# Retention and feed-forward on one core: decay tables made from the first one, and the products of rows 9 to 12 in one piece each

## Chip, cores and metric

One core of one Trainium2 chip. The metric is device time in microseconds of one execution. Engines by short names: PE (TensorE, matrix products), DVE (VectorE), ACT (ScalarE), POOL (GpSimd), SP (SyncE, which only issues transfers here).

## What is computed

The first half is a linear attention with a decaying state, the second a feed-forward layer on its result:

```python
B, H, S, D = 4, 8, 768, 64
gamma = 1.0 - 2.0 ** (-5.0 - np.arange(H))
for t in range(S):
    state = gamma * state + k[t] (outer) v[t]            # per batch and head, 64 x 64
    y[t] = (q[t] @ state) / sqrt(D)
x = y.transpose(0, 2, 1, 3).reshape(B * S, H * D)        # 3072 tokens x 512
h = x @ w_in                                             # 512 -> 2048
g = h * clip(h + 3, 0, 6) / 6
out = g @ w_out                                          # 2048 -> 512
```

The weights arrive as 64-bit floats, and the kernel makes 32-bit ones of them.

## The kernel before

**Rows.** The 3072 tokens are 24 rows of 128 tokens (6 rows per batch). The loop over time is done row by row as matrix products: scores of q and k within a row (`sc`), the product of the masked scores and v (`y`, the inner part), q times the state of the rows before (`y`, the past part), and k times v added to a running sum `uz`. The sum lies in PSUM; before it is used or goes on, ACT copies it into a tile `state` (function `keep`, L462). Decays are not applied to the state: k, v and y are multiplied by powers of gamma. Rows 0 to 7 multiply y at the end, by a table `early["dq"][:, r]` of 128 x 512 numbers (step x, L609); since y has to be multiplied by gamma to the power of the place in the batch, there are six such tables, one per row of a batch. Later rows multiply q beforehand, on POOL.

**The six tables.** The host hands in `bits`, six rows of bfloat16 parts; one PE product of 6 x 128 by 6 x 512 gives a table in PSUM (step T, L559), and ACT (tables 0, 1, 4, 5: `COPIED`) or DVE (tables 2, 3) copies it into SBUF (step C, L563 and L565). `bits` lies in the memory that the split weights of `w1` take later, so the first step that writes `w1` there (u0: ACT, L219, `w<-ww`) waits for the last product that reads `bits`.

**Rows 8 and on** are done in two halves (chunks of 64 tokens). The second half of row r-1 is added to `uz`, with the past part of that half-row's y beside it: this is step P (the first part of the products, 16 small matmuls, which the trace shows as 32). Step J is `keep(2r)`, the ACT copy of `uz`. Step Q (`chunk_rest`) is the rest: scores of row r, the inner part of row r-1, and at its end the sum of the first half of row r, which is written into `uz` again; so the end of Q can only run when J has read `uz`. Step K is `keep(2r+1)`. For rows 13 and on these run as one piece, `chunk_burst`:

```python
together(lists["add"][0], lists["past"][0])     # P
if lists["add"][0]:
    keep(2 * r)                                 # J
chunk_rest(lists)                               # Q
```

**The feed-forward layer** runs on the same PE: `h` is made of 12 matmuls of 128 x 512 per tile (step h, L505, three at a time), ACT makes relu6's first half (step r, L512), DVE the rest (step g, L516), and `g` goes to device memory (`gd`). The stores are issued from ACT's queue behind the next step r (`to_memory`, L539). There are three buffers for `g`, so a step r waits until the store of the third tile before it has landed.

**The order.** What each engine does in the first stage, about 150 us long, is written out by hand in the table `HEAD` (a letter for the step, a number for the row or tile), which `step` (L547 to L637) walks from left to right; each engine then executes its share in that order and waits on the others by semaphores. Steps a b e q f w convert a piece of the weights `w_in` (DVE, with e on ACT, L183 to L206), u and v split it into two 32-bit parts (ACT L219, DVE L222), c and d multiply v and k by decays (POOL, or four ACT activations of 128 x 64 each, L360), m masks the scores (DVE, L381), X and l split x (ACT, DVE), L and F are loads from SP's queue.

Of the kernel before, what the change touches and what calls it, by code (L numbers as in the profile page):

```python
# [20 lines left out]
P = 128  # L21
# [10 lines left out]
def retention_ffn(ctx: ExitStack, tc: tile.TileContext, qkv, w_in, w_out, dvs, dkc, dqc, dmc, tab, out, B, H, S, D):  # L32
# [22 lines left out]
    ONPOOL = (0, 1)  # L55
    COPIED = (0, 1, 4, 5)
    HEAD = """
        L0 L1 F L2 F L3 L4 O0 c0 T0 m0.0 T1 C0 T2 d0 m0.1 C1 T3 C2 N0 O1 x0 c1 U0 d1 m1.0 T4 B0 U1 a0 Y1 b0 e0 m1.1 X0
        q0 N1 f0 F L5 L6 L7 c2 O2 w0 B1 x1 d2 Y2 m2.1 u0 m2.0 U2 a1 N2 B2 l0 X1 b1 T5 C3 c3 O3 x2 d3 Y3 m3.1 m3.0 e1
        U3 l1 N3 B3 q1 C4 O4 c4 x3 f1 F Y4 d4 m4.1 m4.0 X3 U4 X2 v0 O5 B4 w1 C5 N4 l2 c5 a2 Y5 l3 d5 m5.0 x4 e2 s6  # L60
        m5.1 h0.0 c6 b2 N5 f2 d6 q2 F h0.0 u1 m6 p6 x5 h0.0 A6 X4 v1 S7 c7 w2 h0.0 a3 X5 m7 h0.1 u2 b3 l5 y6 h0.1 v2
        B6 e3 q3 p7 h0.1 l4 A7 d7 h0.1 f3 F h0.2 x6 r0.0 w3 i7 X6 u3 y7 h0.2 x7 h0.2 g0.0 X7 v3 h0.2 r0.1 l6 B7 h0.3
        l7 L8 h0.3 a4 h1.0 b4 e4 g0.1 h1.0 r0.2 q4 h1.0 f4 F h1.0 w4 h1.1 g0.2 u4 h0.3 a5 r1.0 v4 h1.1 g1.0 h0.3 b5
        h0.4 r0.3 q5 h0.4 e5 h0.4 f5 F h0.4 g0.3 Q8 L9 w5 a6 h1.1 K8 b6 r0.4 q6 h1.1 u5 P9 e6 h1.2 r1.1 h1.2 J9 g1.1
        h1.2 m8 h1.2 f6 F h1.3 v5 h1.3 w6 h1.3 g0.4 u6 h1.3 r1.2 v6 h1.4 r1.3 a7 h1.4 b7 e7 Q9 g1.2 q7 g1.3 h1.4 f7 F
        h1.4 w7 h1.5 a8 u7 b8 h1.5 e8 q8 h1.5 K9 f8 F L10 r1.4 h0.5 g1.4 h1.5 v7 h1.6 w8 h0.5 a9 u8 h0.5 b9 r1.5 q9
        h0.5 v8 h1.6 g1.5 h1.6 h1.6 P10 r1.6 h1.7 e9 h0.6 J10 f9 F r0.5 h0.6 m9 h1.7 g0.5 h0.6 g1.6 h1.7 w9 h1.7 a10
        b10 h0.6 r1.7 q10 h0.7 u9 e10 Q10 v9 r0.6 f10 F w10 h1.8 a11 u10 h0.7 b11 X8 q11 h0.7 e11 g1.7 h0.7 K10 g0.6
        X9 h1.8 v10 r0.7 h1.8 f11 F L11 h0.8 w11 h0.8 g0.7 h1.8 a12 l8 h0.8 r1.8 h0.8 g1.8 h1.9 r0.8 h1.9 u11 g0.8 e12
        h1.9 v11 h1.9 f12 P11 m10 h1.10 b12 h1.10 q12 F h1.10 l9 h1.10 w12 h1.11 a13 u12 b13 h1.11 J11 v12 r1.9 h1.11  # L70
        e13 g1.9 h1.11 r1.10 q13 Q11 f13 F L12 g1.10 w13 h1.12 X10 m11 h0.9 K11 u13 l10 h1.12 a14 h0.9 b14 e14 q14
        h0.9 r1.11 f14 h1.12 g1.11 P12 v13 h1.12 J12 w14 h0.9 a15 h0.10 u14 b15 r1.12 h0.10 e15 v14 h0.10 r0.9 h0.10
        g1.12 h0.11 r0.10 q15 h0.11 f15 h0.11 g0.9 h0.11 w15 h0.12 g0.10 u15 h0.12 r0.11 v15 h0.12 g0.11 h0.12 Q12
        r0.12 g0.12 h0.13 K12 m12 X11 h0.13 l11 h0.13 h0.13 h0.14 r0.13 h0.14 g0.13 h0.14 h0.14 h0.15 r0.14 h0.15
        g0.14 h0.15 h0.15 h1.13 r0.15 h1.13 g0.15 h1.13 h1.13 h1.14 r1.13 h1.14 g1.13 h1.14 h1.14 h1.15 r1.14 h1.15
        g1.14 h1.15 h1.15 r1.15 g1.15
    """
    BUFS = {"lkt": 1, "lqt": 2, "lvn": 2, "lkn": 1}
    SPARE = ("lkn", "lkt", "lqt", "lqt")
# [462 lines left out]
    def head():  # L542
# [4 lines left out]
        def step(kind, *a):  # L547
            r = a[0] if a else 0
            if kind == "L":
                load(r)  # L550
                if r == AHEAD:
                    nc.sync.dma_start(out=cmask, in_=dmc)
                if r < AHEAD:
                    rows[r]["dq"] = early["dq"][:, r % ROWS_B]
            elif kind == "F":
                fetched.append(fetch(w_in[len(fetched)], 2))
            elif kind == "T":
                tables[r] = ps_h.tile([P, UT], F32, tag="h", name=nm("t"))
                nc.tensor.matmul(tables[r], bits[:, 0:P], bits[:, P + r * UT : P + (r + 1) * UT], start=True, stop=True)  # L559
            elif kind == "C":  # L560
                to, src = early["dq"][:, r].rearrange("p a n -> p (a n)"), tables.pop(r)
                if r in COPIED:
                    nc.scalar.activation(out=to, in_=src, func=AF.Copy)  # L563
                else:
                    nc.vector.tensor_copy(out=to, in_=src)  # L565
            elif kind == "z":
                if "spare" not in both:
                    both["spare"] = h_bank()
                for _ in range(r):
                    nc.tensor.matmul(both["spare"][:, 0:BLK], mask[:, 0], mask, start=True, stop=True)  # L570
            elif kind == "O":
                whole_scores(r)
            elif kind == "N":
                whole_inner(r)
            elif kind == "Y":
                whole_past(r)
            elif kind == "U":
                whole_sums(r)
            elif kind == "s":
                together(*scores(r))  # L580
            elif kind == "S":
                for pair in zip(scores(r), inners(r - 1)):
                    together(*pair)
            elif kind == "i":
                for todo in inners(r):
                    together(todo)
            elif kind in "py":
                sums(r, "py".index(kind), "qt")
            elif kind in "AB":
                keep(2 * r + 1 + "AB".index(kind))  # L590
            elif kind == "P":
                lists = later(r)
                together(lists["add"][0], lists["past"][0])
            elif kind == "Q":
                chunk_rest(later(r))
            elif kind in "JK":
                keep(2 * r + "JK".index(kind))
            elif kind in "cd":
                decay(r, "cd".index(kind))
            elif kind == "m":  # L600
                if r < WHOLE:
                    whole_weigh(*a)
                elif r < AHEAD:
                    weigh(r, r % 2, tri)
                else:
                    weigh(r, 0, cmask)
            elif kind == "x":
                t = rows[r]["x"] = apool.tile([P, NPAIR, P], F32, tag="xr", name=nm("xr"))
                nc.vector.tensor_tensor(out=t, in0=both["y"][:, r % 2], in1=rows[r]["dq"], op=ALU.mult)  # L609
            elif kind == "X":  # L610
                high(x_place(r)[0], rows[r]["x"] if r < AHEAD else both["y"][:, r % 2])
            elif kind == "l":
                low(x_place(r)[1], x_place(r)[0], rows[r]["x"] if r < AHEAD else both["y"][:, r % 2])
                del rows[r]
            elif kind in "abeqf":
                if r not in conv:
                    conv[r] = conversion(fetched[r])
                conv[r][kind]()
# [203 lines left out]
def constants(H, S, D):  # L822
# [89 lines left out]
```

## Time and profile before

| | |
|---|---|
| device time, three runs | 571.28, 571.71, 572.10 us (median 571.71) |
| the profiled execution | 572.05 us, of it 570.3 us span |
| PE busy | 563.5 us, 99% of the span |
| DVE / ACT / POOL busy | 429.6 / 249.2 / 44.2 us |
| chain that ended last, by engine | PE 94%, DVE 3%, DMA 1% |

The chain that ended last is the list of pieces of work, followed back from the last instruction, each of which released the next; a microsecond can be won where it is in this chain. The first 52 us are the only stretch where engines other than PE are in it for long.

### The profile page before, as it was taken

The page shows a single profiled execution, that of the slowest core. Times are in us where ns is not written, and L with a number is a line of the kernel's source. Part 1 is how long each engine was busy: PE and PEld are TensorE (multiplying, and loading weights), DVE is VectorE, ACT ScalarE, POOL GpSimd, SP SyncE. Part 2 cuts the span into 40 slices and gives each one's busy share as a digit, 9 for nine tenths or more (in the row PEclk, how much of TensorE's full clock was granted, in tenths as well). Part 3 has the DMA queues.
Part 4 walks back from the last instruction along what each step waited for, and adds up shares of the span by engine and source line. Part 5 has one row for each costly group of instructions (what it writes and reads, how often), then busy time and mean ns, then how long its engine had stood idle before and what let it go on. Part 6 is the DMA issues. An engine that isn't in the chain of part 4 may idle for free.

```text
span 570.3 us, 11862 instructions
## 1 busy us (share of the span) xinstructions
PE 563.5 (99%) x4832; PEld 462.6 (81%) x4832; DVE 429.6 (75%) x594; ACT 249.2 (44%) x388; POOL 44.2 (8%) x50
## 2 busy tenths in 40 slices
PE   8999999999999999999999999999999999999997
PEld 6777888888888888888888888888888888888885
DVE  5879879942777678887737989679776698676881
ACT  4863434532444443444434654444335443344430
POOL 3001110220111111122000000000000000000000
PEclk9999999999999999999999999999999999999999
DMA  8946787762656666667543485565744747636611
GB/s 314 369 140 220 232 278 228 259 227 92 220 206 223 216 223 215 231 231 260 165 161 115 150 292 189 175 226 167 263 165 132 240 162 258 206 115 189 213 75 74
DMA packets 60626, 115.68 MB, mean 203 GB/s; under 512 B 6166, under 2 KB 6934, under 8 KB 60572
## 3 DMA queue, kind: packets, MB, share of 16 engines
q1 hardware_dynamic: 46304, 89.54, 47.8%
q10 hardware_dynamic: 14268, 25.39, 11.7%
q8 instruction: 38, 0.62, 0.5%
q14 instruction: 16, 0.13, 0.1%
HBM read 83.45 MB, written 31.46 MB: 201 GB/s over the span
## 4 chain that ended last, share of the span: by engine, by line
PE 94%; DVE 3%; DMA 1%; ACT 0%; issue 0%; SPq 0%; DVEq 0%
PE h L505 45%; PE o L782 40%; PE uz L458 3%; PE y L458 3%; PE sc L458 2%; DMA early<-in_qkv 1%; DMA st<-in_w_in 1%; DVE we L200 1%; DVE x L222 0%; DVE am L381 0%; DVE w L222 0%; DVE g L516 0%; DVE wb L187 0%; DVE xr L609 0%; DVE wb L195 0%
## 5 line engine op out<-in xcount | busy, mean ns | idle before, releaser
L505 PE MATMUL h<-x,w 128*128 128x512 f32 x1152 | 270.1, 393 | 0.2
L505 PEld LDWEIGHTS h<-x,w 128*128 128x128 f32 x1152 | 213.9, 188 | 46.4 <-DVE w L222 0.6
L782 PE MATMUL o<-gc,w 128*128 128x512 f32 x1008 | 228.6, 389 | 0.0
L782 PEld LDWEIGHTS o<-gc,w 128*128 128x128 f32 x1008 | 189.2, 188 | 39.3
L512 ACT ACTIVATE g<-h,three 128x512 f32<-128x512 f32 x96 | 65.8, 687 | 109.7 <-PE h L505 81.1
L516 DVE SCALAR_TENSOR_TENSOR g<-g,h 128x512 f32<-128x512 f32 x96 | 65.5, 684 | 56.2 <-ACT g L512 56.0
L219 ACT ACTIVATE gc<-gv 128x1024 fp32r<-128x1024 f32 x48 | 50.9, 1060 | 61.0 <-PE o L782 55.2
L222 DVE TENSOR_TENSOR gc<-gv,gc 128x1024 fp32r<-128x1024 f32 x48 | 58.7, 1222 | 22.5 <-ACT gc L219 22.5
L219 ACT ACTIVATE gc<-spare 128x1024 fp32r<-128x1024 f32 x36 | 38.2, 1061 | 50.3 <-PE o L782 43.3
L222 DVE TENSOR_TENSOR gc<-spare,gc 128x1024 fp32r<-128x1024 f32 x36 | 44.0, 1221 | 10.1 <-ACT gc L219 10.0
L192 ACT ACTIVATE we<-we,ebias 128x512 int32<-128x512 int32 x32 | 23.0, 719 | 17.1 <-DVE we L183 16.3
L219 ACT ACTIVATE w<-ww 128x384 fp32r<-128x384 f32 (+2 forms) x34 | 18.6, 552 | 24.9 <-DVE ww L206 20.6
L200 DVE SCALAR_TENSOR_TENSOR we<-st,we 128x512 int32<-128x512 int32 x32 | 23.0, 720 | 2.3 <-ACT we L192 2.2
L195 DVE SCALAR_TENSOR_TENSOR wb<-st,wb 128x512 f32<-128x512 uint32 x32 | 23.0, 720 | 0.7
L347 POOL TENSOR_TENSOR qs<-qt,dq 128x512 f32<-128x512 f32 x16 | 23.0, 1439 | 6.3 <-DMA dq<-in_decays_q 6.3
L206 DVE SCALAR_TENSOR_TENSOR ww<-wb,we 128x512 f32<-128x512 f32 x32 | 22.9, 715 | 0.8
L462 ACT ACTIVATE state<-uz 128x256 f32<-128x256 f32 x39 | 14.8, 379 | 19.5 <-PE y L458 9.7
L222 DVE TENSOR_TENSOR w<-ww,w 128x384 fp32r<-128x384 f32 (+2 forms) x34 | 20.4, 604 | 1.5 <-ACT w L219 1.4
L136 DVE TENSOR_TENSOR spare<-spare,gv 128x1024 f32<-128x1024 f32 x12 | 14.7, 1223 | 6.1 <-DMA gv<-gd 6.0
L343 POOL TENSOR_TENSOR kn<-kn,ccst 128x512 f32<-128x512 f32 x8 | 9.0, 1128 | 120.9 <-DMA kn<-in_qkv 85.0
L458 PE MATMUL y<-qs,state 64*64 64x64 f32 x480 | 18.3, 222 | 0.0
L458 PE MATMUL y<-am,vn 64*64 64x64 f32 x512 | 18.1, 219 | 0.0
(69 smaller groups left out, 417.9 us busy)
## 6 DMA issues: line engine op xcount, KB each, us to landing
gd<-g ACTq DMA_DIRECT2D x96, 256.0 KB, 2.9
gv<-gd SPq DMA_DIRECT2D x48, 512.0 KB, 4.7
gv<-gd SPq DMA_DIRECT2D x48, 256.0 KB, 3.0
st<-in_w_in SPq DMA_DIRECT2D x32, 256.0 KB, 3.9
st<-in_w_out SPq DMA_DIRECT2D x16, 512.0 KB, 5.8
early<-in_qkv SPq DMA_DIRECT2D x28, 256.0 KB, 4.6
kt<-in_qkv SPq DMA_DIRECT2D x16, 256.0 KB, 3.5
qt<-in_qkv SPq DMA_DIRECT2D x16, 256.0 KB, 3.9
```

The costliest lines, as they stand in the source:

```text
L192: nc.scalar.activation(out=t["e"], in_=t["e"], func=AF.Relu, scale=8.0, bias=ebias)
L195: nc.vector.scalar_tensor_tensor(out=t["b"].bitcast(F32), in0=lo.bitcast(U32), scalar=2.0**-32, in1=t["b"], op0=ALU.mult, op1=ALU.add)
L200: nc.vector.scalar_tensor_tensor(out=t["e"], in0=hi, scalar=-2147483648, in1=t["e"], op0=ALU.bitwise_and, op1=ALU.bitwise_or)
L206: nc.vector.scalar_tensor_tensor(out=t["w"], in0=t["b"].bitcast(F32), scalar=2.0**-20, in1=t["e"].bitcast(F32), op0=ALU.mult, op1=ALU.mult)
L219: nc.scalar.activation(out=hi, in_=src, func=AF.Copy)
L222: nc.vector.tensor_tensor(out=lo, in0=src, in1=hi, op=ALU.subtract)
L347: nc.gpsimd.tensor_tensor(out=t["qs"], in0=t["qt"], in1=d, op=ALU.mult)
L458: nc.tensor.matmul(out_, lhs, rhs, start=start, stop=True, skip_group_check=True)
L505: nc.tensor.matmul(h, t[:, o, a], xs[u][b][:, k], start=k + n == 0, stop=(k, n) == (NK - 1, 2), skip_group_check=True)
L512: return g, nc.scalar.activation(out=g, in_=h, func=AF.Relu, bias=three).ins
L516: ins = nc.vector.scalar_tensor_tensor(out=g, in0=g, scalar=6.0, in1=h, op0=ALU.min, op1=ALU.mult)
L782: nc.tensor.matmul(acc[i][h] if last else acc[i][:, h], w2c[j][:, RIGHT[i], x, h], gc[:, y, jj], start=j == 0 and n == 0, stop=j == NFP - ...
```

## The change

Two things. First, of the six tables only the first is made by a product of `bits` and copied (ACT). Table r is then table 0 times one factor per head, gamma to the power 128 r, from five rows that ride along with the decays of v (`vcst` becomes part of `vtab`, 20 columns wider): tables 1, 4 and 5 by four ACT activations of 128 x 128 each with a factor per partition, tables 2 and 3 by one DVE product of 128 x 512. Steps C4 and C5 move forward to before u0. `bits` shrinks from 6 x 1600 to 6 x 320 words. Second, for rows 9 to 12 the words P and J move to directly ahead of Q.

```diff
-        ... T0 m0.0 T1 C0 T2 d0 m0.1 C1 T3 C2 N0 O1 x0 c1 U0 d1 m1.0 T4 B0 ... d2 Y2 m2.1 u0 ... T5 C3 ... C4 O4 ... C5 N4
+        ... T0 m0.0 C0 d0 m0.1 C1 C2 N0 O1 x0 c1 U0 d1 m1.0 B0 ... d2 C4 C5 Y2 m2.1 u0 ... C3 ... O4 ... N4
...
-        h0.4 ... u5 P9 e6 h1.2 r1.1 h1.2 J9 g1.1 ... r1.3 a7 h1.4 b7 e7 Q9
+        h0.4 ... u5 e6 h1.2 r1.1 h1.2 g1.1 ... r1.3 a7 h1.4 b7 e7 P9 J9 Q9
...
-    vcst = const.tile([P, WHOLE, H], F32, name="vcst")
-    nc.scalar.dma_start(out=vcst.rearrange("p n h -> p (n h)"), in_=dvs)
+    vtab = const.tile([P, WHOLE * H + (ROWS_B - 1) * NPAIR], F32, name="vtab")
+    nc.scalar.dma_start(out=vtab, in_=dvs)
+    vcst = vtab[:, 0 : WHOLE * H].rearrange("p (n h) -> p n h", h=H)
+    later_by = vtab[:, WHOLE * H :].rearrange("p (n h) -> p n h", h=NPAIR)
...
-                nc.tensor.matmul(tables[r], bits[:, 0:P], bits[:, P + r * UT : P + (r + 1) * UT], start=True, stop=True)
+                nc.tensor.matmul(tables[r], bits[:, 0:P], bits[:, P:], start=True, stop=True)
             elif kind == "C":
-                to, src = early["dq"][:, r].rearrange("p a n -> p (a n)"), tables.pop(r)
-                if r in COPIED:
-                    nc.scalar.activation(out=to, in_=src, func=AF.Copy)
+                to, of = early["dq"][:, r], early["dq"][:, 0]
+                if not r:
+                    nc.scalar.activation(out=to.rearrange("p a n -> p (a n)"), in_=tables.pop(r), func=AF.Copy)
+                elif r in COPIED:
+                    for p in range(NPAIR):
+                        nc.scalar.activation(out=to[:, p], in_=of[:, p], func=AF.Copy, scale=later_by[:, r - 1, p : p + 1])
                 else:
-                    nc.vector.tensor_copy(out=to, in_=src)
+                    by = later_by[:, r - 1, :, None].to_broadcast([P, NPAIR, P])
+                    nc.vector.tensor_tensor(out=to, in0=of, in1=by, op=ALU.mult)
```

P10 to P12 and J10 to J12 are moved in the same way as P9 and J9. The lines of the changed kernel are one to five higher than those before (`keep` is L463, relu L513, the stores L540).

**First place: ACT around u0**, the first split of weights (`w<-ww`; `early_152` is v of rows 2 and 3, `early_136` the tables, `state` the copies of `uz`, `x` the split of a finished row, `we` a step of the conversion). Before:

```order
L462 ACTIVATE state_315<-uz 128x256
L360 ACTIVATE early_152<-early_152,vcst 128x64 x4
L219 ACTIVATE w_24_314<-ww_312 128x4x128
L462 ACTIVATE state_352<-uz 128x256
L219 ACTIVATE x_264<-xr_317 128x4x128
L360 ACTIVATE early_152<-early_152,vcst 128x64 x8
L192 ACTIVATE we_342<-we_342,ebias 128x512
L462 ACTIVATE state_415<-uz 128x256
L563 ACTIVATE early_136<-t_238 128x512
```

With the change:

```order
L463 ACTIVATE state_310<-uz 128x256
L361 ACTIVATE early_152<-early_152,vtab 128x64 x4
L567 ACTIVATE early_136<-early_136,vtab 128x128 x8
L220 ACTIVATE w_20_309<-ww_307 128x4x128
L463 ACTIVATE state_355<-uz 128x256
L220 ACTIVATE x_259<-xr_312 128x4x128
L361 ACTIVATE early_152<-early_152,vtab 128x64 x8
L193 ACTIVATE we_345<-we_345,ebias 128x512
L463 ACTIVATE state_416<-uz 128x256
```

Eight activations of 128 x 128 (tables 4 and 5) stand ahead of u0, and the copies of these tables, of which the last row of before shows the first, are gone from where they stood.

**Second place: ACT between row 8 and row 9** (`g` tiles are steps r, `DMA gd<-g` the stores; `state_946`, now `state_994`, is J9). Before:

```order
L192 ACTIVATE we_903<-we_903,ebias 128x512
L512 ACTIVATE g_941<-h_818,three 128x512
L462 ACTIVATE state_946<-uz 128x256
L219 ACTIVATE w_56_710<-ww_968 128x4x128
L512 ACTIVATE g_978<-h_937,three 128x512
L539 DMA gd_67<-g_941 128x512
L539 DMA gd_69<-g_912 128x512
L512 ACTIVATE g_987<-h_960,three 128x512
L192 ACTIVATE we_989<-we_989,ebias 128x512
L219 ACTIVATE w_103_1060<-ww_1058 128x4x128
```

With the change:

```order
L193 ACTIVATE we_902<-we_902,ebias 128x512
L513 ACTIVATE g_924<-h_817,three 128x512
L220 ACTIVATE w_51_709<-ww_949 128x4x128
L513 ACTIVATE g_959<-h_920,three 128x512
L540 DMA gd_67<-g_924 128x512
L540 DMA gd_69<-g_911 128x512
L513 ACTIVATE g_968<-h_941,three 128x512
L193 ACTIVATE we_970<-we_970,ebias 128x512
L463 ACTIVATE state_994<-uz 128x256
L220 ACTIVATE w_98_1059<-ww_1057 128x4x128
```

J9 has moved from behind r1.1 to behind r1.3 (`g_987`, now `g_968`) and e7. In the same way J10 moves from behind e9 to behind r1.7, its stores, a split and e10; J11 from behind u12 to behind r1.10 and its store; and J12 from behind r1.11 to behind r0.11 and its two stores.

**Third place: PE around P10** (`uz` and `y` are the first two rows of P10's eight, `h` steps of the feed-forward layer). Before:

```order
L505 MATMUL h_1110<-x_587,w_56_710 128x512 x3
L505 MATMUL h_1101<-x_264,w_56_710 128x512 x9
L505 MATMUL h_1110<-x_587,w_56_710 128x512 x9
L458 MATMUL uz<-vn_893,am_137 64x64 x2
L458 MATMUL y_138<-qs_899,state_946 64x64 x2
```

With the change:

```order
L506 MATMUL h_1147<-x_586,w_98_1059 128x512 x3
L506 MATMUL h_1152<-x_259,w_51_709 128x512 x6
L506 MATMUL h_1147<-x_586,w_98_1059 128x512 x3
L506 MATMUL h_1152<-x_259,w_51_709 128x512 x3
L506 MATMUL h_1147<-x_586,w_98_1059 128x512 x6
L506 MATMUL h_1152<-x_259,w_51_709 128x512 x3
L506 MATMUL h_1194<-x_259,w_98_1059 128x512 x3
L459 MATMUL uz<-vn_892,am_137 64x64 x2
L459 MATMUL y_138<-qs_898,state_994 64x64 x2
```

P10 has moved past 27 matmuls of the feed-forward layer (P9, P11 and P12 past 30, 24 and 42) and now ends where Q10 begins. Otherwise PE loses five table products; the orders on POOL and SP stay as they were.


## Rows read from the trace of the kernel before

**Rows 1.** The page: the shares of the chain that ended last, by engine.

```profile
PE 94%; DVE 3%; DMA 1%; ACT 0%; issue 0%; SPq 0%; DVEq 0%
```

**Rows 2.** The chain that ended last, in order of time, from 17 to 53 us: start, length, what.

```profile
17.67 0.63 ACT w L219
...
22.31 0.69 DVE xr L609
...
28.32 1.15 PE sc L458 x32
...
52.43 2.56 PE h L505 x10
```

**Rows 3.** ACT in order of time, 10 to 22 us: start, busy time, instruction, in brackets the idle time before it and what ended it.

```profile
10.13 0.38 ACT L462 ACTIVATE state<-uz 128x256 f32<-128x256 f32 x1 [2.61 <-PE uz L458]
...
13.88 1.05 ACT L360 ACTIVATE early<-early,vcst 128x64 f32<-128x64 f32 x4
17.67 0.63 ACT L219 ACTIVATE w<-ww 128x512 fp32r<-128x512 f32 x1 [2.74 <-PE t L559]
18.21 0.37 ACT L462 ACTIVATE state<-uz 128x256 f32<-128x256 f32 x1
18.47 0.62 ACT L219 ACTIVATE x<-xr 128x512 fp32r<-128x512 f32 x1
18.99 2.01 ACT L360 ACTIVATE early<-early,vcst 128x64 f32<-128x64 f32 x8
20.90 0.71 ACT L192 ACTIVATE we<-we,ebias 128x512 int32<-128x512 int32 x1
```

**Rows 4.** PE in order of time, 7 to 11 us, with the same columns.

```profile
7.38 1.26 PE L458 MATMUL y<-am,early 128*64 128x128 f32 x16
...
10.02 0.38 PE L559 MATMUL t<-bits 6*128 6x512 bf16 x1
10.61 0.69 PE L458 MATMUL uz<-early,kn 128*64 128x64 f32 x16 [0.21 <-issue]
```

**Rows 5.** DVE in order of time, 6 to 23 us.

```profile
6.21 1.29 DVE L381 TENSOR_TENSOR am<-sc,mask 128x512 f32<-128x512 f32 x2 [3.61 <-issue]
7.41 0.68 DVE L565 COPY early<-t 128x512 f32<-128x512 f32 x1
...
22.31 0.69 DVE L609 TENSOR_TENSOR xr<-y,early 128x512 f32<-128x512 f32 x1 [1.28 <-PE y L458]
```

**Rows 6.** The chain again, 58 to 158 us: PE alone, at the beginnings of P and Q and of the feed-forward products behind them. P9 at 58.12, Q9 at 65.77, Q10 at 84.06, Q11 at 102.36, Q12 at 118.60, the whole piece of a later row at 155.31.

```profile
58.12 0.20 PE uz L458 x2
...
58.75 7.02 PE h L505 x30
65.77 0.20 PE sc L458 x2
...
67.35 9.74 PE h L505 x42
...
84.06 0.20 PE sc L458 x2
...
102.36 0.20 PE sc L458 x2
...
118.60 0.20 PE sc L458 x2
...
155.31 0.20 PE uz L458 x2
...
157.35 2.72 PE h L505 x11
```

**Rows 7.** PE in order of time, inside Q9: the first matmul pair that writes `uz` again.

```profile
66.68 0.24 PE L458 MATMUL uz<-vn,am 64*64 64x64 f32 x2
```

**Rows 8.** ACT in order of time around Q9 (ACTq is ACT's issuing of a transfer), 59 to 70 us.

```profile
62.77 0.33 ACTq L539 DMA_DIRECT2D gd<-g  x1
...
63.19 0.39 ACTq L539 DMA_DIRECT2D gd<-g  x1
66.59 0.69 ACT L512 ACTIVATE g<-h,three 128x512 f32<-128x512 f32 x1 [2.79 <-DMA gd<-g]
67.18 0.71 ACT L192 ACTIVATE we<-we,ebias 128x512 int32<-128x512 int32 x1
69.38 0.64 ACT L219 ACTIVATE w<-ww 128x512 fp32r<-128x512 f32 x1 [1.49 <-DVE ww L206]
```

**Rows 9.** ACT in order of time around Q10, 82 to 86 us.

```profile
82.74 0.69 ACT L512 ACTIVATE g<-h,three 128x512 f32<-128x512 f32 x1 [3.12 <-PE h L505]
82.80 1.51 ACTq L539 DMA_DIRECT2D gd<-g  x2
...
85.51 0.68 ACT L512 ACTIVATE g<-h,three 128x512 f32<-128x512 f32 x1
```

**Rows 10.** ACT in order of time around Q11 and Q12, 101 to 120 us.

```profile
101.90 0.68 ACT L512 ACTIVATE g<-h,three 128x512 f32<-128x512 f32 x1
...
118.22 0.69 ACT L512 ACTIVATE g<-h,three 128x512 f32<-128x512 f32 x1 [0.95 <-DMA gd<-g]
118.24 1.45 ACTq L539 DMA_DIRECT2D gd<-g  x2
```

**Rows 11.** The page's table of transfers, the stores of `g`: count, KB each, median us from issue to landing.

```profile
gd<-g ACTq DMA_DIRECT2D x96, 256.0 KB, 2.9
```

More of the change, by code (lines that the diff above doesn't have):

```diff
@@ L57, in retention_ffn @@
     HEAD = """
[L58 to L76, printed above, removed]
+        L0 L1 F L2 F L3 L4 O0 c0 T0 m0.0 C0 d0 m0.1 C1 C2 N0 O1 x0 c1 U0 d1 m1.0 B0 U1 a0 Y1 b0 e0 m1.1 X0 q0 N1 f0 F L5
@@ new lines, in retention_ffn @@
+        L6 L7 c2 O2 w0 B1 x1 d2 C4 C5 Y2 m2.1 u0 m2.0 U2 a1 N2 B2 l0 X1 b1 C3 c3 O3 x2 d3 Y3 m3.1 m3.0 e1 U3 l1 N3 B3 q1 O4
+        c4 x3 f1 F Y4 d4 m4.1 m4.0 X3 U4 X2 v0 O5 B4 w1 N4 l2 c5 a2 Y5 l3 d5 m5.0 x4 e2 s6 m5.1 h0.0 c6 b2 N5 f2 d6
+        q2 F h0.0 u1 m6 p6 x5 h0.0 A6 X4 v1 S7 c7 w2 h0.0 a3 X5 m7 h0.1 u2 b3 l5 y6 h0.1 v2 B6 e3 q3 p7 h0.1 l4 A7 d7
+        h0.1 f3 F h0.2 x6 r0.0 w3 i7 X6 u3 y7 h0.2 x7 h0.2 g0.0 X7 v3 h0.2 r0.1 l6 B7 h0.3 l7 L8 h0.3 a4 h1.0 b4 e4 g0.1
+        h1.0 r0.2 q4 h1.0 f4 F h1.0 w4 h1.1 g0.2 u4 h0.3 a5 r1.0 v4 h1.1 g1.0 h0.3 b5 h0.4 r0.3 q5 h0.4 e5 h0.4 f5 F
@@ new lines, in retention_ffn @@
+        h0.4 g0.3 Q8 L9 w5 a6 h1.1 K8 b6 r0.4 q6 h1.1 u5 e6 h1.2 r1.1 h1.2 g1.1 h1.2 m8 h1.2 f6 F h1.3 v5 h1.3 w6 h1.3
+        g0.4 u6 h1.3 r1.2 v6 h1.4 r1.3 a7 h1.4 b7 e7 P9 J9 Q9 g1.2 q7 g1.3 h1.4 f7 F h1.4 w7 h1.5 a8 u7 b8 h1.5 e8 q8
+        h1.5 K9 f8 F L10 r1.4 h0.5 g1.4 h1.5 v7 h1.6 w8 h0.5 a9 u8 h0.5 b9 r1.5 q9 h0.5 v8 h1.6 g1.5 h1.6 h1.6 r1.6 h1.7
+        e9 h0.6 f9 F r0.5 h0.6 m9 h1.7 g0.5 h0.6 g1.6 h1.7 w9 h1.7 a10 b10 h0.6 r1.7 q10 h0.7 u9 e10 P10 J10 Q10 v9 r0.6
+        f10 F w10 h1.8 a11 u10 h0.7 b11 X8 q11 h0.7 e11 g1.7 h0.7 K10 g0.6 X9 h1.8 v10 r0.7 h1.8 f11 F L11 h0.8 w11 h0.8
@@ new lines, in retention_ffn @@
+        g0.7 h1.8 a12 l8 h0.8 r1.8 h0.8 g1.8 h1.9 r0.8 h1.9 u11 g0.8 e12 h1.9 v11 h1.9 f12 m10 h1.10 b12 h1.10 q12 F
+        h1.10 l9 h1.10 w12 h1.11 a13 u12 b13 h1.11 v12 r1.9 h1.11 e13 g1.9 h1.11 r1.10 q13 P11 J11 Q11 f13 F L12 g1.10
+        w13 h1.12 X10 m11 h0.9 K11 u13 l10 h1.12 a14 h0.9 b14 e14 q14 h0.9 r1.11 f14 h1.12 g1.11 v13 h1.12 w14 h0.9 a15
+        h0.10 u14 b15 r1.12 h0.10 e15 v14 h0.10 r0.9 h0.10 g1.12 h0.11 r0.10 q15 h0.11 f15 h0.11 g0.9 h0.11 w15 h0.12
+        g0.10 u15 h0.12 r0.11 v15 h0.12 g0.11 h0.12 P12 J12 Q12 r0.12 g0.12 h0.13 K12 m12 X11 h0.13 l11 h0.13 h0.13
@@ L77, in retention_ffn @@
+        h0.14 r0.13 h0.14 g0.13 h0.14 h0.14 h0.15 r0.14 h0.15 g0.14 h0.15 h0.15 h1.13 r0.15 h1.13 g0.15 h1.13 h1.13
+        h1.14 r1.13 h1.14 g1.13 h1.14 h1.14 h1.15 r1.14 h1.15 g1.14 h1.15 h1.15 r1.15 g1.15
     """
@@ L118, in retention_ffn @@
     cmask = const.tile([P, NPAIR * D], F32, name="cmask")
-    const.tile([P, 40], F32, name="edge")
+    const.tile([P, 16], F32, name="edge")
     ebias = const.tile([P, 1], F32, name="ebias")
@@ L827, in constants @@
     dv = by_side((g ** -t[:WHOLE, :, None])[:, :, None], H)[:, :, 0].transpose(1, 0, 2).reshape(P, -1)
+    by = np.stack([g[1::2], g[0::2]])[:, None] ** (P * np.arange(1, S // P))[:, None]
+    dv = np.concatenate([dv, np.repeat(by.reshape(2, -1), D, axis=0)], axis=1)
     dk = (g ** -t[:, :, None]).reshape(S // P, 2, D, H // 2, 2).transpose(4, 2, 0, 1, 3).reshape(P, -1)
@@ L830, in constants @@
     qc = np.broadcast_to(qc, (S // P, H // 2, 2, D, P)).transpose(0, 2, 3, 1, 4).reshape(S // P, 2 * D, -1)
-    dq = np.roll(qc, D, axis=1).reshape(S // P, 2, D, H // 2 * P)[:, :, 0].transpose(1, 0, 2).reshape(2, -1)
+    dq = np.roll(qc, D, axis=1).reshape(S // P, 2, D, H // 2 * P)[0, :, 0]
     parts = []
```

## The prediction, made before the run

> **What bounds the kernel.** I read the page first: of the chain that ended last PE holds 94%, DVE 3% and ACT as good as nothing [rows 1]. So only two kinds of place can matter: the first 52 us, where other engines stand in the chain, and the places behind them where an edit makes PE wait. Then I read the chain itself. Up to 52.43 us it goes back and forth between PE, ACT and DVE [rows 2]; from there on PE works without a gap, and P and Q of rows 9 to 12 are pieces of its unbroken work [rows 6]. In that second stretch, work taken from PE counts in full, and any wait put in counts in full. Last I read ACT, PE and DVE in order of time around each edit [rows 3 to 5, 7 to 10].
>
> **Tables 1 to 4, nothing.** Of the four products ahead of the first y the first stays. That y starts at 7.38, but it needs the masked scores, and DVE ends these at 6.21 + 1.29 = 7.50 [rows 4, 5]. So three products less leave it where it is. The product at 10.02 is covered too: the uz behind it, at 10.61, comes 0.10 us after ACT's copy of `uz` ended (10.13 + 0.38 = 10.51) [rows 3, 4]. DVE's copy of 0.68 us becomes a DVE product of the same 128 x 512; such products take 0.68 to 0.69 [rows 5]. Table 1 now takes ACT four activations behind the copy of table 0, and ACT then waits 2.61 us for PE anyway [rows 3]. Without these covers the four products, of 0.38 us each [rows 4], would give back 1.5 us.
>
> **Table 5 and u0, −0.47 us.** Here a table product is in the chain: ACT, which has been idle for 2.74 us, starts u0 when it is done, at 17.67, since u0 writes where `bits` lies [rows 2, 3]. From there it goes on through the state copy, y, a wait of DVE of 1.28 us for that y (22.31), and DVE's work to the PE of 28.32 and 52.43 [rows 2, 5]. With the change no late product reads `bits`, and the idle time takes the eight activations of tables 4 and 5. The last activation ahead of them starts its successor at 13.88 + 4 x 0.245 = 14.86. What one of 128 x 128 takes no row shows. The 128 x 64 kind goes at (20.90 − 18.99)/8 = 0.24 us, and a copy of 128 x 256 at 18.47 − 18.21 = 0.26 in a sequence and 0.37 to 0.38 by itself [rows 3]. I take 0.29, nearest to the 128 x 64 kind, which has a factor per partition as well, and a little more for its columns: 8 x 0.29 = 2.3, so u0 starts at 17.2 and everything behind it 0.47 us sooner. With 0.24 it is 0.9 sooner, with 0.38 it is 17.90, 0.23 later. The chain behind 22.31 is DVE's until PE takes over, and PE's from 28.32 on, so I let the whole of it through. The two copies of 0.5 us that ACT loses later are slack.
>
> The Trainium skill, ScalarE: Activation LUTs, section Rules for kernel authors, speaks against this edit: it gives a product to VectorE, and budgets some 0.3 us per activation with a pointer operand plus 0.83 ns per element. By that budget, an estimate from that page, one activation of 128 columns takes 0.41 us, u0 starts at 18.1, and this term is +0.44. The trace has 0.24 us for 64 columns where the page would have 0.35, so I hold to the rows; the case is a rival below.
>
> **The four merges, −0.68 us.** P9 takes 58.75 − 58.12 = 0.63 and Q9 takes 67.35 − 65.77 = 1.58, together 2.21; the same work in one piece takes 157.35 − 155.31 = 2.04 [rows 6]. That is 0.17 us for each of four, all on PE.
>
> **J9 behind r1.3, +1.76 us.** Between P and the end of Q now stands a state copy J, and ACT executes it where the new order has it. Merged, the piece of row 9 begins at 65.77 − 0.63 = 65.14. It writes `uz` again 0.67 us before its end, as Q9 does (66.68 of 67.35) [rows 6, 7]: at 65.14 + 2.04 − 0.67 = 66.51 it must have J9. Now J9 is queued behind r1.3 and e7. But r1.3 waits 2.79 us for a store of `g`, issued at 62.77, and starts at 66.59 [rows 8]. Then e7 starts at 67.18 and takes 0.71, the next begins 0.10 ahead of its end (as 18.47 does, of 18.21 + 0.37 [rows 3]), so J9 starts at 67.79 and takes 0.38; with the 0.10 to PE it is 68.27. PE waits 68.27 − 66.51 = 1.76 us. If the store landed 2.9 us behind its issue, as the median does [rows 11], instead of 3.8, it would be 0.84. All of this moves with the 0.47 us alike. Behind J9 on ACT stands u7, which waited 1.49 us for DVE anyway [rows 8].
>
> **J10 behind r1.7, +0.30 us.** r1.7 starts when its h is done, at 82.74, and Q10 began 84.06 − 82.74 = 1.32 later [rows 6, 9]. P10 will begin there and want J10 1.37 later, at 2.69 behind r1.7. On ACT two stores are issued behind r1.7 (1.51 us), then a split and e10, and the next instruction starts at 85.51, 2.77 behind it; with J10's 0.37 and 0.10 that is 3.24. PE waits 0.55. But two stores in a row also took 0.33 and 0.39 [rows 8]; then it waits for nothing. I take 0.30, and 0 and 0.55 as ends.
>
> **J11 and J12, nothing.** J11 follows r1.10 (101.90), so it is done by about 103.0; it is wanted at 102.36 − 0.63 + 1.37 = 103.10 and later by PE's lateness [rows 6, 10]. J12 follows r0.11 and its stores: 118.24 + 1.45 + 0.38 + 0.10 = 120.17, against 118.60 − 0.63 + 1.37 = 119.34 [rows 6, 10]. That would be 0.83 of waiting, but PE is some 1.5 us late by then (1.76 + 0.30 − 3 x 0.17), while r0.11 waits for a store rather than for PE.
>
> **Sum.** −0.47 − 0.68 + 1.76 + 0.30 = +0.91 us, on the profiled execution's 572.05 (0.34 above the median): 572.96, or 572.6 on the median of 571.71. A measurement of this kernel tells some 0.2%, 1.14 us, from no change, so this is within it.
>
> **Rivals.**
> - *No wait for J.* If the stores land sooner and ACT reaches each J in time, the two gains stand alone: −0.47 − 0.68 = −1.15, 570.6. For it: the median landing of 2.9 us, and that r1.3 is one wait among many that can slide. Against it: 1.76 is more than the 0.9 that the store could give back, and J12's 0.83 waits behind it for a PE that is not late. Chance 0.22.
> - *J12 waits too.* Should the stores and ACT's steps all shift with PE after the wait at Q9, PE's lateness does not cover J12, and Q12 adds 0.83: +1.74, 573.4. It decides where ACT reaches r0.11 more than about 0.7 us later than before. For it: from Q10 on ACT also waits for PE (3.12 us at r1.7); against it, r0.11 waits for a store. Chance 0.18.
> - *The head loses.* If an activation of 128 x 128 takes as long as a lone state copy, 0.38 us, u0 comes 0.23 later instead of 0.47 earlier: +1.61, 573.3. Chance 0.08. The Trainium skill's budget, the rule told above, would make it +0.44 at this place, and the trace so far speaks against it.
> - *All removed PE time counts.* Five products of 0.38 us and the 0.68, with no wait: −2.58, 569.1. The order shows that the products are gone; but the rows show four of them covered. Chance 0.07.
>
> The forecast itself has 0.45; with its ends (the head 0.23 less to 0.4 more, J10 at 0 or 0.55) it is 572.0 to 573.1. Range: from the rival without waits to the one with J12, 570.5 to 573.6. Faster: the last rival and half of the first, 0.18. Slower: J12, the head, and 0.08 of the forecast, 0.34. Else 0.48.
>
> **What would show it.** In the trace of the changed kernel: u0 at about 17.2 us behind eight activations of 0.29; the first unbroken PE work at about 52.0 instead of 52.43; in the piece of row 9 a wait of PE for `state` of some 1.8 us, with r1.3 ahead of it waiting for a store; one of 0 to 0.55 in row 10; none in rows 11 and 12; the pieces themselves at 2.04 plus that wait. No `state` wait on PE in row 9, or u0 later than 17.67, would make the forecast wrong.

## The result and the profile after

The changed kernel takes 574.9 us (median of 7 runs, 573.56 to 577.03); its ratio to the kernel before is 1.0054, interval 1.0041 to 1.0067, so 2.3 to 3.8 us slower. The forecast was 572.6 us and no difference. The ratio leaves out one execution of the kernel before that took 801.3 us; its other six took 571.28 to 572.45. The profiled execution has 574.89 us, 573.2 of them span, which is 2.9 more than before.

The page of the changed kernel, as [rows 1] of before:

```profile
PE 92%; DMA 4%; DVE 1%; issue 1%; SPq 0%; POOL 0%; DVEq 0%; POOLq 0%
```

PE's part of the chain has shrunk from 94% to 92%, and that of transfers has grown from 1% to 4%. This overstates what stands between PE's pieces: where PE waits, the chain is followed back through loads that ran while PE was still at work (58.52 to 65.10 in the chain below). The waits themselves say more. What PE waited for (engine, line, releaser: total us, times, longest):

```profile
PE uz L459 <- issue: 3.7, 3, 1.7
```

No such row of 3.7 us exists before. The releaser "issue" means that no visible event ended these waits; the next views show by time which it was. The chain, start and length, answering to [rows 6]:

```profile
55.51 1.10 PE sc L459 x32
...
58.52 6.58 DMA dq<-in_decays_q
65.12 0.59 POOL am L344
65.71 1.43 POOL qs L348
67.14 1.61 issue
68.74 0.27 PE uz L459 x2
...
69.44 15.87 PE h L506 x69
85.31 0.20 PE uz L459 x2
...
87.35 15.91 PE h L506 x69
103.25 0.20 PE uz L459 x2
...
104.81 1.39 issue
106.20 0.27 PE uz L459 x2
...
106.90 13.82 PE h L506 x60
...
122.31 0.27 PE uz L459 x2
123.00 21.99 PE h L506 x96
```

The pieces of rows 9 to 12 end at 69.44, 87.35, 106.90 and 123.00; before, Q9 ended at 67.35 [rows 6], and Q10 to Q12, in the same view, at 85.64, 103.93 and 120.17. Set against each other this is the account of the two profiles:

| stretch | later than before at its end | its own part | forecast |
|---|---|---|---|
| up to the scores of row 8 (54.98 before, 55.51 now) | +0.53 | +0.53 | −0.47 |
| row 9 | +2.09 | +1.56 | +1.59 |
| row 10 | +1.71 | −0.38 | +0.13 |
| row 11 | +2.97 | +1.26 | −0.17 |
| row 12 | +2.83 | −0.14 | −0.17 |

Row 9 is as foreseen. Three lines are not: the head, row 10, which became cheaper and waited for nothing, and above all row 11.

In row 9 the chain comes from POOL's decayed q (`qs`, done at 67.14), since "issue" names nothing that ended later. Whether PE waits for POOL or for J9 is settled by an experiment below.

ACT around row 9, answering to [rows 8]:

```profile
63.55 0.33 ACTq L540 DMA_DIRECT2D gd<-g  x1
...
63.97 0.39 ACTq L540 DMA_DIRECT2D gd<-g  x1
67.07 0.69 ACT L513 ACTIVATE g<-h,three 128x512 f32<-128x512 f32 x1 [2.75 <-DMA gd<-g]
67.66 0.71 ACT L193 ACTIVATE we<-we,ebias 128x512 int32<-128x512 int32 x1
68.27 0.37 ACT L463 ACTIVATE state<-uz 128x256 f32<-128x256 f32 x1
69.85 0.63 ACT L220 ACTIVATE w<-ww 128x512 fp32r<-128x512 f32 x1 [1.21 <-DVE ww L207]
```

J9 ends at 68.64, and PE's uz goes on at 68.74: "issue" is J9, behind r1.3 and e7, behind a store that lands 3.5 us after its issue. All of it as the prediction had it, the 0.10 us to PE included.

ACT ahead of row 11, in the changed kernel:

```profile
95.13 0.69 ACT L513 ACTIVATE g<-h,three 128x512 f32<-128x512 f32 x1 [0.67 <-PE h L506]
97.26 0.33 ACTq L540 DMA_DIRECT2D gd<-g  x1
97.63 0.63 ACT L220 ACTIVATE w<-ww 128x512 fp32r<-128x512 f32 x1 [1.80 <-DMA st<-in_w_in]
...
103.30 0.63 ACT L220 ACTIVATE w<-ww 128x512 fp32r<-128x512 f32 x1 [4.42 <-DVE ww L207]
...
105.02 0.68 ACT L513 ACTIVATE g<-h,three 128x512 f32<-128x512 f32 x1
105.29 0.33 ACTq L540 DMA_DIRECT2D gd<-g  x1
105.72 0.39 ACT L463 ACTIVATE state<-uz 128x256 f32<-128x256 f32 x1
```

and the same place before:

```profile
94.41 0.69 ACT L512 ACTIVATE g<-h,three 128x512 f32<-128x512 f32 x1 [1.69 <-DMA gd<-g]
94.43 0.34 ACTq L539 DMA_DIRECT2D gd<-g  x1
94.99 0.62 ACT L219 ACTIVATE w<-ww 128x512 fp32r<-128x512 f32 x1
...
99.91 0.63 ACT L219 ACTIVATE w<-ww 128x512 fp32r<-128x512 f32 x1 [3.69 <-DVE ww L206]
```

Behind r0.8 (95.13) stands a store of g, behind it u11 (97.63). Before, the store was issued at once and u11 followed 0.58 us behind r0.8. Now the store is issued 2.1 us behind r0.8, and what the trace names for the wait of ACT is a load of weights (`st<-in_w_in`) on SP's queue. u11 is 2.6 us later than before, DVE's next conversion and u12 (103.30) 3.4 us, and J11 (105.72) stands behind u12: PE waits 1.39 us for it. The order with each instruction's waits tells why a store waits for a load. Before, and with the change:

```order
L539 DMA gd_71<-g_1353 128x512 [waits DVE_49]
```

```order
L540 DMA gd_71<-g_1352 128x512 [waits DMAHW3_49,DVE_49]
```

All 370 transfers of the program, whichever engine issues them, take turns on eight completion counters (DMAHW0 to 7), and one that comes to a counter waits until the transfer that used it last has landed. The turns are fixed when the program is built, in one sequence over all engines. With row 10 in one piece this store has its turn two places later, behind SP's loads of `am` and `dq`, and so comes to counter 3, which a load of weights used last. Of the seventeen programs of this document the nine with row 10 in one piece give the store this wait, and the other eight do not. The diff doesn't show it, and neither does the order without its waits.

### The profile page after: what moved, and what is told of

It is laid out like the page before. It is cut to its first block, busy times and chain, and to the rows that moved or that the text cites. A ratio compares the mean times of both kernels' runs of the same rounds, so it can differ in the third digit from the quotient of the medians.

```text
span 573.2 us, 11865 instructions
## 1 busy us (share of the span) xinstructions
PE 562.2 (98%) x4827; PEld 463.4 (81%) x4827; DVE 422.6 (74%) x594; ACT 251.9 (44%) x397; POOL 43.4 (8%) x50
## 4 chain that ended last, share of the span: by engine, by line
PE 92%; DMA 4%; DVE 1%; issue 1%; SPq 0%; POOL 0%; DVEq 0%; POOLq 0%
PE h L506 45%; PE o L787 40%; PE uz L459 3%; PE y L459 3%; PE sc L459 2%; DMA st<-in_w_in 2%; DMA dq<-in_decays_q 1%; DMA early<-in_qkv 1%; SPq L158 0%; DVE x L223 0%; DVE am L382 0%; POOL qs L348 0%; DVE xr L614 0%; DVE early L570 0%; DVE w L223 0%
## 5 line engine op out<-in xcount | busy, mean ns | idle before, releaser
L513 ACT ACTIVATE g<-h,three 128x512 f32<-128x512 f32 x96 | 66.0, 687 | 113.6 <-PE h L506 83.4
L463 ACT ACTIVATE state<-uz 128x256 f32<-128x256 f32 x39 | 14.8, 380 | 19.5 <-PE y L459 9.5
L140 DVE TENSOR_TENSOR spare<-gv 128x1024 f32<-128x1024 f32 x12 | 14.7, 1222 | 5.1 <-DMA gv<-gd 5.1
```

The lines of the kernel that those rows point to most:

```text
L513: return g, nc.scalar.activation(out=g, in_=h, func=AF.Relu, bias=three).ins
```

## The experiments

All are compared with the kernel before on the same chip. "Wait" in the texts is how much longer a piece in the profile is than 2.11 us, which whole pieces take there from first start to last end.

**The tables alone.** The changed kernel with P and J of rows 9 to 12 back where they were, of which the diff shows row 9:

```diff
-        h1.1 u5 e6 h1.2 r1.1 h1.2 g1.1 ... e7 P9 J9 Q9
+        h1.1 u5 P9 e6 h1.2 r1.1 h1.2 J9 g1.1 ... e7 Q9
...
```

> Only the tables: five of six made from the first, C4 and C5 ahead of u0, bits and vtab as in the change; P and J of rows 9 to 12 stay where they were. Theory 1 (what the prediction said of the head): u0 starts sooner and the run is 0.47 us shorter than before. Theory 2 (from the trace of the changed kernel): the transfer of the decays of k, 128 x 48, is issued at 1.9 us instead of 3.8, in front of the loads of rows 0 and 1, and one load of row 1 waits for the transfer of vtab, so all loads land 0.5 to 1.2 us later; the head ends later and the run is 0.3 to 1.0 us longer. Theory 3: the late head of the changed kernel's profile was one execution's accident; then no difference, within 0.3 us.

Measured 0.9988 (0.9980 to 0.9996): 0.7 us faster (0.2 to 1.1). That fits theory 1; of theory 3's difference of at most 0.3 us only the edge lies in the interval. The profile shows u0 where the prediction put it, at 17.2:

```profile
13.94 1.05 ACT L361 ACTIVATE early<-early,vtab 128x64 f32<-128x64 f32 x4
14.89 2.44 ACT L567 ACTIVATE early<-early,vtab 128x128 f32<-128x128 f32 x8
17.23 0.62 ACT L220 ACTIVATE w<-ww 128x512 fp32r<-128x512 f32 x1
```

Eight activations take 2.34 us, 0.29 each, the value taken for lack of a row. The early transfer of k's decays is there too in this kernel, which is faster all the same. The changed kernel's own profile has u0 more than a microsecond later, though the activations take the same time:

```profile
16.16 2.44 ACT L567 ACTIVATE early<-early,vtab 128x128 f32<-128x128 f32 x8
18.50 0.62 ACT L220 ACTIVATE w<-ww 128x512 fp32r<-128x512 f32 x1
```

The head moves that much between executions of either kind. The scores of row 8 start at 53.98 to 55.68 in the eight profiles with the tables of before and at 53.94 to 55.97 in the nine with the new ones. So the 0.53 us that the changed kernel's profile lost in the head cannot be laid to the change. PE's first 32 small matmuls already differ, in the kernel before, the tables alone, and the changed kernel:

```profile
5.18 0.90 PE L458 MATMUL sc<-early 64*64 64x128 f32 x32
```

```profile
5.82 1.01 PE L459 MATMUL sc<-early 64*64 64x128 f32 x32
```

```profile
5.82 1.56 PE L459 MATMUL sc<-early 64*64 64x128 f32 x32
```

**The merges, together and one by one.** On the code of before, row 9 shown, rows 10 to 12 in the same way:

```diff
-        h1.1 u5 P9 e6 h1.2 r1.1 h1.2 J9 g1.1 ... e7 Q9
+        h1.1 u5 e6 h1.2 r1.1 h1.2 g1.1 ... e7 P9 J9 Q9
...
```

> Only the merges of rows 9 to 12, with the six tables made by products as before. The prediction's terms give +1.76 + 0.30 - 0.68 = +1.4 us, with a wait of PE in row 9 alone or nearly. The rival from the trace of the changed kernel gives +2.4 us: a wait of some 1.7 us in row 9 and one of some 1.4 us in row 11, each piece 0.4 us cheaper than in two parts.

> The kernel before with only row 9 in one piece: P9 and J9 directly ahead of Q9. Both theories: PE waits some 1.7 us in row 9 for J9, which stands behind r1.3 and e7; +1.4 to +1.6 us in all. If later slack on other engines took it back, it would be under 0.5 us.

> The kernel before with only row 10 in one piece. The prediction's terms: 0.30 - 0.17 = +0.1 us (0.55 of waiting at most). The rival: no wait in row 10 and the piece 0.4 us cheaper, -0.4 us; but with row 10 in one piece the stores of g and the loads behind it are issued in another order on their eight completion counters, so that one store, some 10 us behind row 10, waits on ACT for a load to land; with J11 where it was before, that should cost PE nothing.

> The kernel before with only row 11 in one piece, J11 behind r1.9, e13 and r1.10 as in the change; the stores and loads keep the order of before, so the store ahead of u11 waits for no load. The prediction's term: no wait for J11, -0.2 to -0.4 us. Theory 1 agrees: the wait of row 11 in the changed kernel needs the late u11. Rival (J11's place alone makes the wait): a wait of 1 us or more in row 11, +0.7 or more.

> The kernel before with only row 12 in one piece, J12 behind r0.11 and its two stores. PE is not late here, since rows 9 to 11 are as before. The prediction's rows give a wait of 0.83 us, less 0.2 to 0.4 for the piece: +0.4 to +0.7 us. If a store ahead of r0.11 lands sooner than in the profile of before: down to -0.4.

| in one piece | ratio (interval) | wait in rows 9, 10, 11, 12, us |
|---|---|---|
| 9 to 12 | 1.0055 (1.0033 to 1.0077) | 1.9, 0, 1.3, 0 |
| 9 | 1.0039 (1.0024 to 1.0055) | 2.4 in row 9 |
| 10 | 1.0007 (0.9998 to 1.0016) | 0 in row 10 |
| 11 | 0.9995 (0.9985 to 1.0005) | 0 in row 11 |
| 12 | 0.9991 (0.9981 to 1.0001) | 0.3 in row 12 |

The four alone and the tables add up to +0.0020, 1.1 us (by their intervals give or take some 1.4), close to the forecast's +0.91. The changed kernel has 1.0054. So the terms were about right one by one, and what was missing is something that happens only where several are together. Row 11 alone waits for nothing, in its place behind r1.10; row 10 alone has the late u11 (the store there waits for the load, 2.1 us), but J11 is early then, and row 11's two parts pay 0.35 us.

**Rows 10 and 11, and all but row 10.** The first on the code of before (row 10 shown, row 11 likewise), the second on the changed kernel:

```diff
-        h1.6 P10 r1.6 h1.7 e9 h0.6 J10 f9 ... u9 e10 Q10
+        h1.6 r1.6 h1.7 e9 h0.6 f9 ... u9 e10 P10 J10 Q10
```

```diff
-        h1.6 r1.6 h1.7 e9 h0.6 f9 ... u9 e10 P10 J10 Q10
+        h1.6 P10 r1.6 h1.7 e9 h0.6 J10 f9 ... u9 e10 Q10
```

> The kernel before with rows 10 and 11 in one piece each, rows 9 and 12 in two. Theory 1 (row 10's merge puts the load of weights ahead of the store of g, ACT waits for that load ahead of u11, and J11 comes late): a wait of 1 to 1.6 us in row 11, though PE is not late from row 9; +0.3 to +0.9 us (two pieces at 0.4 us less, a wait more). Theory 2 (it is the wait of row 9 that makes ACT late in row 11): no wait in row 11, -0.6 to -0.8.

> The changed kernel with row 10 back in two pieces; rows 9, 11 and 12 and the tables as in the change. Stores and loads have the order of before. Theory 1: the wait of row 9 stays, 1.7 us, that of row 11 is gone; PE is late enough that J12 is in time: -0.7 for the tables, +1.6 for row 9, -0.4 each for rows 11 and 12, so +0.1 us, 3 us less than the changed kernel. Theory 2: both waits stay, +1.3 or more.

Rows 10 and 11 give 1.0052 (1.0034 to 1.0069), 3.0 us, with no merge in row 9. All but row 10 gives 1.0002 (0.9992 to 1.0011), 2.9 us less than the changed kernel, with waits of 2.1, 0 and 0 us in rows 9, 11 and 12 (in a profiled execution of 576.0 us, 3.5 above the median; the last section has more on it). Theory 1 holds, and its price was too low: with rows 10 and 11, ACT waits longer for the load, and PE waits 0.8 us in row 10 and twice in row 11, 3.4 us in all, once for DVE's late split of a finished row as well (ACT, then PE):

```profile
98.09 0.63 ACT L218 ACTIVATE w<-ww 128x512 fp32r<-128x512 f32 x1 [3.21 <-DMA st<-in_w_in]
```

```profile
103.44 0.27 PE L457 MATMUL y<-qs,state 64*64 64x64 f32 x2 [1.12 <-DVE x L221]
...
106.84 0.27 PE L457 MATMUL uz<-vn,am 64*64 64x64 f32 x2 [1.78 <-issue]
```

**J9 first.** The same edit to the kernel with row 9 alone in one piece, on the code of before, and to the changed kernel:

```diff
-        h1.4 r1.3 a7 h1.4 b7 e7 P9 J9 Q9 g1.2
+        h1.4 a7 h1.4 b7 P9 J9 Q9 r1.3 e7 g1.2
```

> The kernel before with row 9 in one piece, as in the run of row 9 alone, but r1.3 and e7 moved behind Q9, so that J9 stands ahead of them on ACT. Theory 1 (PE waits for J9, and J9 waits behind r1.3, which waits for a store of g): J9 starts as soon as P9 is done, at about 65.8, PE waits for nothing, and the piece is 0.4 us cheaper than in two parts: -0.4 us against before, 2.3 us less than row 9 alone. Theory 2 (PE waits in row 9 for POOL's decayed k or q, since the merged piece comes with them late): r1.3's place does not matter, and it stays +1.5 to +2.2 us.

> The changed kernel with r1.3 and e7 behind Q9. Theory 1: the wait of some 1.7 us in row 9 is gone, 1.5 to 2.0 us less than the changed kernel, so +1.1 to +1.6 us against before. Rival: J11 comes at a time that the loads and DVE set, not PE, so that the wait in row 11 grows by what row 9 gave back, and the time hardly moves: +2.5 to +3.1.

With row 9 alone 0.9996 (0.9987 to 1.0004), and no wait: r1.3 and e7 were the cause, and POOL, whose place did not change, was not. In the changed kernel 1.0029 (1.0018 to 1.0041): 1.4 us less than it, but its profile has waits of 0.5 in row 10 and 1.6 in row 11 (the profiled execution, 571.9 us, is one of the fastest of a kernel with a median of 574.1). The rival was half right: part of what row 9 gives back is waited for again.

**J11 first, then all J first.** On the changed kernel: the first edit by itself, then both together with J9 first:

```diff
-        v12 r1.9 h1.11 e13 g1.9 h1.11 r1.10 q13 P11 J11 Q11 f13
+        v12 h1.11 h1.11 q13 P11 J11 Q11 r1.9 e13 g1.9 r1.10 f13
```

```diff
-        u15 h0.12 r0.11 v15 h0.12 g0.11 h0.12 P12 J12 Q12 r0.12
+        u15 h0.12 v15 h0.12 h0.12 P12 J12 Q12 r0.11 g0.11 r0.12
```

> The changed kernel with r1.9, e13, g1.9 and r1.10 moved behind Q11, so that J11 stands directly behind u12 on ACT as before. The store that waits for a load to land stays as it is in the changed kernel, and u12 stays late. Theory 1 (what costs PE 1.4 us in row 11 is the three instructions between u12 and J11, once ACT is late): wait in row 11 gone or under 0.3 us, 1.0 to 1.4 us less than the changed kernel, +1.7 to +2.1 against before. Rival (u12 alone is so late that J11 is late behind it too): a wait of 0.5 us or more stays, +2.5 or more.

> The changed kernel with J9, J11 and J12 ahead of the relus that delayed them: r1.3 and e7 behind Q9; r1.9, e13, g1.9 and r1.10 behind Q11; r0.11 and g0.11 behind Q12. If the waits for J are the whole loss, what is left are the tables (-0.7 us measured) and four pieces at 0.4 us less: -2.3 us, about 569.6. If the relus behind the pieces hold up the products or the stores instead: -1 to +1.

J11 first gives 1.0023 (1.0009 to 1.0038), as theory 1 had it, and no wait in row 11. But in the profile row 12 waits 2.1 us instead: there J12 stands behind r0.11 and its two stores, whose issue took 1.6 us. That execution took 575.3 us, 1.8 above the median, so not every one need have this wait. All J first gives 1.0006 (0.9995 to 1.0017) where 2.3 us less were expected, a miss: waits of 0.9 in row 10 and 1.1 in row 11 remained. Of the latter 0.7 are for DVE's late split of a finished row, as with rows 10 and 11 alone; and u12 itself was late (102.31), with J11 behind it.

**u11 ahead of the store.** On the changed kernel, and on the one with all J first:

```diff
-        h1.9 r0.8 h1.9 u11 g0.8 e12 h1.9
+        h1.9 h1.9 u11 e12 r0.8 g0.8 h1.9
```

> The changed kernel with r0.8 (and g0.8) moved behind u11 and e12, so that the store which waits for a load to land stands behind u11 on ACT, not ahead of it. J11 stays where the change has it. Theory 1 (that store holds ACT for 1.8 us, u11 and with it DVE's conversion and u12 come late, and J11 behind them): u11 starts 2 to 3 us sooner, the wait of 1.4 us in row 11 is gone or under 0.5, 0.9 to 1.4 us less than the changed kernel, +1.7 to +2.2 against before. Rival (J11 is late for another reason, as by r1.9 and r1.10 themselves): the wait stays over 1 us, +2.7 or more.

> The changed kernel with all of it: J9, J11 and J12 ahead of the relus, and u11 and e12 ahead of r0.8. The run without the last of these had waits of 0.9 us in row 10 and 1.1 in row 11. Theory 1: the wait in row 11 is gone, 0.8 to 1.1 us less than that run, -0.5 to -0.8 against before; a wait in row 10 may stay. Rival (ACT's pace is set by loads and DVE from row 9 on, so that a wait removed comes back in the next row): no change from that run, 0 to +0.6.

On the changed kernel 1.0026 (1.0016 to 1.0037), 1.6 us less than it; the wait in row 11 falls from 1.6 to 0.7, a little less than theory 1 had it. With all J first too, 0.9973 (0.9961 to 0.9985), 1.5 us faster than before; a wait of 0.65 in row 10 stays. There ACT is early, and J11 waits for PE (ACT, the last of the three is J11):

```profile
92.04 0.62 ACT L220 ACTIVATE w<-ww 128x512 fp32r<-128x512 f32 x1
...
98.67 0.63 ACT L220 ACTIVATE w<-ww 128x512 fp32r<-128x512 f32 x1 [4.82 <-DMA gd<-g]
101.93 0.38 ACT L463 ACTIVATE state<-uz 128x256 f32<-128x256 f32 x1 [2.63 <-PE uz L459]
```

**J9 first, without row 10.** On the changed kernel:

```diff
-        h1.6 r1.6 h1.7 e9 h0.6 f9 ... u9 e10 P10 J10 Q10
+        h1.6 P10 r1.6 h1.7 e9 h0.6 J10 f9 ... u9 e10 Q10
...
-        h1.4 r1.3 a7 h1.4 b7 e7 P9 J9 Q9 g1.2
+        h1.4 a7 h1.4 b7 P9 J9 Q9 r1.3 e7 g1.2
```

> As the last, with r1.3 and e7 behind Q9. The wait of row 9 goes too: -0.7 - 3 x 0.4 = -1.9 us, less a wait of up to 0.8 for J12, since PE is not late: -1.1 to -1.9, at least level with the best so far (-1.5).

0.9984 (0.9973 to 0.9996), 0.9 us faster than before: a little short of the expectation, with 0.3 us of waiting for J12. It and the kernel with all J and u11 first beat both kernels of the change, as the tables alone do; the intervals of the three overlap.

## Why the prediction was wrong

- **The head.** The cost was right: 0.29 us per activation, and 0.7 us gained by the tables alone (0.2 to 1.1) where 0.47 stood. That u0 came at 17.23, where 17.2 stood, is partly luck: in the profiles of the other kernels with the new tables it comes at 17.35 to 18.91, with the old ones at 17.39 to 18.47. In the changed kernel's own profile it is at 18.50, later than the 17.67 that the prediction had named as a sign of being wrong. The time of u0 in a single profile was too loose a sign. By the budget of the Trainium skill that was weighed there (ScalarE: Activation LUTs, Rules for kernel authors) the estimate was 0.41 us for each of these activations and a later u0. That is near what one takes by itself here (2.44 − 7 x 0.29 = 0.4), but in a row each starts about 0.1 us before the one ahead of it ends, and 0.29 is what counts.
- **Tables 1 to 4.** Nothing in the runs contradicts "nothing", but no run tests it by itself.
- **The merges' own saving** was too small: row 10, which waited for nothing, became 0.38 us cheaper, not 0.17. The other 0.2 lies in the feed-forward products. 69 of them in one run take 15.87 us, while before 42 and 27 took 9.74 + 6.35 = 16.09: here the break between the two kinds of work cost PE 0.2 us more than the small matmuls themselves show.
- **J9.** Right in its cause, shown by moving r1.3 and e7, and about right in size: 1.59 net forecast, 1.56 in the profile, 1.95 net with row 9 alone (67.35 became 69.30). That 1.59 and 1.56 agree so closely is luck: the piece was 1.95 longer instead of 1.76, and the merge gave back 0.38 instead of 0.17.
- **J10.** Waited for nothing in the changed kernel and with row 10 alone, the lower end. In the four kernels that merge row 10 and row 11 and do not wait in row 9 it waits 0.5 to 0.9 us, more than the 0.30 that was taken.
- **J11 and J12, nothing.** This is the step that failed. In its own terms it was right: row 11 alone waits for nothing. It took ACT's times around row 11 from rows of before and added PE's lateness as a margin. But ACT's times there were changed by the change: row 10's merge gave a store of g a load to wait for, and that held u11, DVE's conversion, u12 and J11 in turn. PE was idle for 1.39 us there, and the piece took 1.6 longer. Shown by leaving row 10 out (the 2.9 us go) and by rows 10 and 11 alone (3.0 us come); that the store is a link of it, by moving u11 ahead of it (1.6 of the 2.9 us go). The rival for J12 was real as a mechanism, in the profile with J11 first, but not in the changed kernel, where PE was late enough; and its price of 0.83 was too high where PE is not late: 0.3 with row 12 alone, where the issue of the two stores took 0.82 us instead of 1.45.
- **The range** failed with that step: no rival had a wait for J11, or a cost that the merge of one row brings to another.

What stays open: how the 2.9 us divide between the wait for J11 (1.39 in the profile's chain) and other things that vary between executions. The changed kernel's seven runs spread over 3.5 us, the six of before over 1.2 (1.6 to 2.9 in larger sets of runs later). One thing that varies is PE's clock behind a wait, in the last section; the kernel without row 10's merge has that too, so it does not account for the 2.9 us.

## What to carry to other kernels

A step that is cheap to run can still be wrong to move: look at what stands ahead of it on its engine and how late that can be, not at how long it takes. Where an edit moves work in a program whose transfers share completion counters, compare the waits of both programs, of the transfers too, for the order alone doesn't show that a store has been given a load to wait for. A wait of PE can cost more than its length, since its clock may fall behind it. And when singly costed edits meet, cost the later ones on the times that the earlier ones leave.

## What the runs showed of the hardware

The same 32 matmuls at the start of the program took 0.90, 1.01 and 1.56 us in three executions, at a granted clock of 1.00 (the upper of the two levels, 2.4 GHz) in all of them between 4 and 8 us; behind them PE's first products came up to 1.3 us later. One profiled execution says little about the first 10 us.

Behind a wait of PE its clock fell in some executions. In the profiled execution of the kernel without row 10's merge PE had been idle for 1.9 us in row 9, up to 69.33, and then went on without a gap; the granted clock fell from 1.00 to 0.50 (the lower level, 1.2 GHz) and was back at 74. Stretch and length, busy time of PE, PEld, DVE, ACT and POOL, granted clock, share of the DMA engines, GB/s:

```profile
66.00:70.00 4.00, 2.13 (x129) 1.95 (x125) 2.63 (x5) 1.57 (x3) 2.17 (x2) 1.00 0.22 84
70.50:73.50 3.00, 3.00 (x8) 2.34 (x7) 2.26 (x5) 2.14 (x4) 0.00 (x0) 0.50 0.57 193
74.00:78.00 4.00, 4.00 (x19) 3.30 (x18) 3.89 (x7) 1.32 (x2) 0.00 (x0) 1.00 0.88 291
```

The 42 products behind that wait took 11.36 us, where they took 9.74 before [rows 6], 1.6 us on top of the wait itself:

```profile
70.02 11.36 PE h L506 x42
```

That the wait is the cause was not tested by itself; a count over all executions speaks for it. A mean clock of 0.996 or 0.997 over the whole execution, as this one had, is on record for 16 of the 77 executions of the eight kernels that have the longest waits of PE in one piece, the changed kernel among them (2 of 7). It is on record for none of the 89 of the other eight kernels with an edit, and for none of the 113 of the kernel before that were run beside them. Where the clock fell in the other 15 is not shown, since only this one was profiled. Where it falls, the prediction's "any wait put in counts in full" is too little.
